# Products of two units at once and a new order of work in an adaLN block with a spectral filter and a SwiGLU FFN

## The chip, the cores and the metric

The kernel runs on one core of a Trainium2 chip. The core has five engines that run side by side, each in the order of its own instructions: TensorE (PE; its weight loads are listed as PEld), VectorE (DVE), ScalarE (ACT), GpSimd (POOL) and SyncE (SP), which here only issues transfers. They wait for one another on semaphores. The metric is the device time of one execution in microseconds (us); lower is better.

## The reference

One block of a transformer with adaptive layer norm. `x` is 2048 x 640, bf16.

```python
mod = (_silu(c) @ w_mod).reshape(c.shape[0], 6, 1, -1)
sa, ca, ga, sb, cb, gb = (mod[:, i] for i in range(6))
h = _layernorm(x) * (1 + ca) + sa
x = x + ga * irfft2(rfft2(h) * (w_r + 1j * w_i)).astype(bf16)     # over both axes
h = _layernorm(x) * (1 + cb) + sb
x = x + gb * ((_silu(h @ w_gate) * (h @ w_up)) @ w_down)          # 640 -> 1728 -> 640
```

## The kernel before

All work is matmuls with tables of cosines and sines. The 2048 rows lie as 16 tiles of 128, the 640 columns as 5 residues of 128. A stage is a set of small functions, one for each step of a tile or unit, and a string `plan` that lists their calls. The order of the plan is the order of the instructions on every engine: an engine never takes an instruction ahead of an earlier one in the plan. Which PSUM buffer a step gets is written out too, in `SLOTS1` and `SLOTS2` (three and four buffers of two banks), and `ON_DVE` names the evictions from PSUM that go to DVE; all others go to ACT. Below, a letter with a number is a call in the plan.

*Forward transform* (some 7 to 36 us). For each tile t: `T` turns x on PE (L301), `h` evicts it (L304), `G` forms a Gram matrix with two more columns of constants (L308), from which `d` takes variance and mean on DVE: a reduce along the diagonal (L313) and a small combination (L315). `p` and `r` make the reciprocal root for two tiles. `s` scales the table of the row transform by it, on POOL (L333, L334; tile 14 on DVE). `B` is the column transform (L340), `Z` evicts it with the mean taken out (DVE, L345), `S` is the row transform's first half (L353, L354) and `A` evicts it into `A_sb` (L367; tile 12 in three pieces, L362 to L364). At the end `J`, `Je` and `N` make turned and negated copies of the filter's weights W_r and W_i. Loads are calls in the plan too: `lx` (x, two tiles), `lg` (row table), `lW0` (W_i) and `lW1` (W_r, 1284 KB each), `lf` (rows of the weights' border), `lsa`, `lga`, `lK`, `lKI`, `lRi` (modulation weights and tables).

*Filter* (36 to 64 us). The 65 columns of the spectrum are 16 units of four and one single. `A_sb` is turned column by column into `B_all`: the first two units by PE (`T0`, `T1`, evicted by `t0`, `t1`, L506 and L507), the others by transposing transfers on SP's queue (`B2` to `B14`, `Bl`). `X` finishes the row transform of two units (L523, L531), `Xe` evicts one. `P` and `R` multiply a unit with W_r and W_i for 48 and 32 of its 80 rows (both L562; 768 and 512 elements). `a` adds the two planes of products on DVE for the units in `ADDED` (L570). `Y` turns the result on PE: 10 matmuls that add the planes (L586, L590), or 5 plain transposes where `a` has added them (L580, L581). `y` evicts (L599). `E` starts the inverse row transform (L611 to L624), `e` evicts into `Ep` (L634), `m` writes mirrored columns (`mirror`, L278). `ga` and `gt` make the gate `ga`, `gs` spreads it over the partitions, `Ri` scales the last table with it (L661).

*Inverse transform and first quarter of the FFN* (64 to 112 us). For each tile: `s` (L720), `V` (L727), `d` (L733), `x` adds the residual into `x1` (L736), `n` and `q` take mean and square sum (L740, L744). The first four tiles are normalized, turned (`T`, L772) and go through `g` (gate and up products, L812), `z` (silu, L817) and `m` (product into `AT`, L821). `sb`, `cb` and `mb` are modulation vectors of 25 small matmuls each (L241), `mt` turns the gate `gb` (L253) and has it spread over all partitions (L262), and `w` (`fold`, L848) multiplies a part of the down weights with it.

*The rest* (112 to 261 us). Down products of a quarter (L934, L921), then the next quarter's gate and up products, without a written plan. `x_out` adds x1 and stores. For the very last half tile the kernel uses two PSUM buffers of 160 columns, adds x1 there with two matmuls by the identity (L931), and evicts with ACT and DVE at once (L946).

Of the kernel before, what the change touches and what calls it, by code (L numbers as in the profile page):

```python
# [19 lines left out]
NI = 160  # L20
# [10 lines left out]
def _tables():  # L31
# [70 lines left out]
    "012021021021021020210210212012010210210210210"  # L102
)
SLOTS2 = (
    "0301321032103213012301230210321023102301230213201231032103210231023102310231320132012310321020130323"
    "013120132013201320132013201320132013201320132013201320132013201320132"
# [4 lines left out]
def adaln_block_kernel(  # L111
# [39 lines left out]
    one11 = const.tile([1, 1], BF16, name="one11")  # L151
    identb = const.tile([P, 128], BF16, name="identb")
# [29 lines left out]
    g_row = [dram.tile([1, D], BF16, name=n) for n in ("ga_row", "gb_row")]  # L182
    nc.vector.memset(one11[:], 1.0)
    nc.vector.memset(eps_t[:], EPS)
    nc.vector.memset(neg1[:], -1.0)
# [32 lines left out]
    def load_g(g):  # L218
# [5 lines left out]
             "lga": load(wm_g[:, :, 0:D], wm_v[:, :, 2 * D:3 * D]), "lRi": load(Rinv_sb[:], Rinv_dram), "lf": fix_rows}  # L224
# [58 lines left out]
    with tc.tile_pool(name="ph1", bufs=3) as ph1, \  # L283
# [33 lines left out]
        def root(t):  # L317
            n = GROUP[t]
            nc.scalar.activation(rstd1[:, t:t + n], vm[:, t:t + n, 0], ACT.Sqrt)
# [75 lines left out]

        cps = Tt[:, 330:330 + NC5]
        for k in range(NC5):
            nc.tensor.matmul(cps[:, k:k + 1], lhsT=c_row[0:1, k * 128:(k + 1) * 128], rhs=one11[:], start=True, stop=True)
        for _ in range(12):
            nc.tensor.matmul(Gt[:, 0:128], lhsT=identb[:], rhs=identb[:], start=True, stop=True)  # L400
# [44 lines left out]
        def negate(i):  # L445
# [5 lines left out]
        S_DVE, S_ACT, T_RING = (14,), (), (1, 2, 3, 4, 5, 6, 7)  # L451
        GROUP = {0: 2, 2: 2, 4: 2, 6: 2, 8: 2, 10: 2, 12: 2, 14: 2}
        plan = (
# [7 lines left out]
        )  # L461
        steps = {**LOADS, "ca": mod_ca, "cb": mod_cb, "rs": r_scaled, "rvp": rv_mm, "rv": rv_out, "T": turn, "h": turned, "G": sums,
# [13 lines left out]
    with tc.tile_pool(name="ph2", bufs=2, reuse_waits="tile") as ph2:  # L476
# [16 lines left out]

        def t2(u):
            ps = pss["t", u] = slot("t2ps")[:, 0, 0:320].bitcast(BF16)
# [97 lines left out]
        def copy_y(u):  # L593
            yf = pss.pop(("y", u))[:].rearrange("p b q -> p (b q)")
            if u in ADDED:
                yf = yf.bitcast(BF16)
# [425 lines left out]
```

## Time and profile before

| | us |
|---|---|
| median of 3 runs | 262.74 (262.62 to 265.64) |
| profiled execution | 262.81 |
| its span, first to last instruction | 261.0 |
| PE busy | 252.7 |
| DVE busy | 141.1 |
| ACT busy | 118.6 |
| POOL busy | 26.4 |

The granted TensorE clock was full throughout. In the timeline a row has start, duration, engine, line, operation, tiles and shapes, with the idle time before it in brackets; in a group (`x16 | 8.7, 550 | 0.0`) the busy time, the mean duration in ns and the idle time before follow the bars. A window's row has its length, then for each engine the busy time and the count of instructions, then clock, DMA share and GB/s. Busy time of PE holds the pipeline's tail of every matmul (a 128-column matmul is listed with 0.22 us), so distances from start to start say more.

### The profile page before, as it was taken

The page shows a single profiled execution, that of the slowest core. Times are in us where ns is not written, and L with a number is a line of the kernel's source. Part 1 is how long each engine was busy: PE and PEld are TensorE (multiplying, and loading weights), DVE is VectorE, ACT ScalarE, POOL GpSimd, SP SyncE. Part 2 cuts the span into 40 slices and gives each one's busy share as a digit, 9 for nine tenths or more (in the row PEclk, how much of TensorE's full clock was granted, in tenths as well). Part 3 has the DMA queues.
Part 4 walks back from the last instruction along what each step waited for, and adds up shares of the span by engine and source line. Part 5 has one row for each costly group of instructions (what it writes and reads, how often), then busy time and mean ns, then how long its engine had stood idle before and what let it go on. Part 6 is the DMA issues. An engine that isn't in the chain of part 4 may idle for free.

```text
span 261.0 us, 5283 instructions
## 1 busy us (share of the span) xinstructions
PE 252.7 (97%) x2168; PEld 159.9 (61%) x2172; DVE 141.1 (54%) x353; ACT 118.6 (45%) x212; POOL 26.4 (10%) x57
## 2 busy tenths in 40 slices
PE   6899999999999999999999999999999999999995
PEld 5788666888995444466544456744445664444664
DVE  5799989999887664933243343234344322433122
ACT  5689879996993669420222222032223103222000
POOL 4289700000010001300000000000000000000000
PEclk9999999999999999999999999999999999999999
DMA  7999499999599100141100040210005011000011
GB/s 243 381 356 298 112 175 160 176 330 379 153 370 303 38 14 1 23 77 57 58 10 3 0 92 11 75 35 10 3 0 100 30 48 35 10 3 0 0 53 50
DMA packets 36798, 27.88 MB, mean 107 GB/s; under 512 B 19493, under 2 KB 34214, under 8 KB 36646
## 3 DMA queue, kind: packets, MB, share of 16 engines
q1 hardware_dynamic: 36762, 27.54, 37.1%
q8 instruction: 17, 0.28, 0.5%
q14 instruction: 7, 0.06, 0.1%
q10 hardware_dynamic: 12, 0.00, 0.0%
HBM read 20.13 MB, written 2.62 MB: 87 GB/s over the span
## 4 chain that ended last, share of the span: by engine, by line
PE 79%; DVE 12%; ACT 3%; issue 2%; DMA 2%; SPq 1%; DVEq 0%; ACTq 0%
PE gu L812 37%; PE oa L934 21%; PE va L720 3%; DVE PP L562 3%; DMA x_sb<-in_A_x_dram 2%; PE oab L733 2%; PE gu L799 2%; ACT junk L744 2%; PE aps L353 1%; DVE AT L821 1%; PE aps L354 1%; PE z L340 1%; DVE Z L345 1%; PE gps L308 1%; DVE late L848 1%
## 5 line engine op out<-in xcount | busy, mean ns | idle before, releaser
L821 DVE TENSOR_TENSOR AT<-gu,sg 128x512 bf16<-128x512 f32 x52 | 35.7, 690 | 63.3 <-ACT sg L817 63.3
L812 PE MATMUL gu<-h2T_all,Wg 128*128 128x512 bf16 x260 | 64.6, 379 | 0.1
L812 PE MATMUL gu<-h2T_all,Wu 128*128 128x512 bf16 x256 | 63.7, 379 | 0.1
L817 ACT ACTIVATE sg<-gu 128x512 f32<-128x512 f32 x52 | 30.7, 596 | 67.9 <-PE gu L812 65.1
L934 PE MATMUL oa<-late,AT 128*128 128x320 bf16 x403 | 56.3, 299 | 0.5 <-DVE AT L821 0.5
L934 PEld LDWEIGHTS <-AT 128*128 128x128 bf16 x429 | 40.7, 98 | 17.6 <-issue 1.1
L812 PEld LDWEIGHTS <-Wu 128*128 128x128 bf16 x260 | 25.4, 98 | 30.7
L812 PEld LDWEIGHTS <-Wg 128*128 128x128 bf16 x260 | 25.3, 98 | 29.9
L948 DVE TENSOR_TENSOR xo<-oa,late 128x320 bf16<-128x320 f32 x31 | 13.4, 484 | 34.6 <-PE oa L934 18.2
L801 ACT ACTIVATE sg<-gu 64x512 f32<-64x512 f32 x4 | 2.4, 591 | 36.0 <-PE gu L799 36.0
L736 DVE SCALAR_TENSOR_TENSOR late<-oab,x_sb 128x640 bf16<-128x640 f32 x16 | 12.8, 822 | 6.4 <-PE oab L733 5.0
L333 POOL TENSOR_SCALAR Gs<-Gtab,rstd 128x256 bf16<-128x256 bf16 x15 | 13.9, 928 | 8.1 <-DVE rstd L323 7.1
L345 DVE SCALAR_TENSOR_TENSOR Z<-rtile,vm,z 128x640 bf16<-128x640 f32 x16 | 13.9, 871 | 0.1
L744 ACT ACTIVATE junk<-late,mean 128x640 bf16<-128x640 bf16 x16 | 13.3, 828 | 0.3
L367 ACT CAST A_sb<-aps 128x650 bf16<-128x650 f32 x15 | 10.6, 706 | 2.1 <-PE aps L354 2.0
L727 ACT CAST VT<-va 128x640 bf16<-128x640 f32 x16 | 10.2, 699 | 1.9 <-PE va L720 1.8
L720 PE MATMUL va<-Htab,Ep 128*128 128x128 bf16 x160 | 10.6, 219 | 0.1
L720 PEld LDWEIGHTS <-Ep 128*128 128x128 bf16 x160 | 9.5, 118 | 0.4 <-DVE Ep L278 0.3
L353 PE MATMUL aps<-Z,Gs 128*128 128x325 bf16 x32 | 9.2, 303 | 0.2 <-DVE Z L345 0.2
L354 PE MATMUL aps<-Z,Gs 128*128 128x315 bf16 x32 | 9.2, 298 | 0.0
L540 ACT CAST X<-xps 128x640 bf16<-128x640 f32 x13 | 8.5, 710 | 1.1 <-PE xps L531 0.8
L562 DVE TENSOR_TENSOR PP<-X,Wb 128x768 bf16<-128x768 bf16 x16 | 8.7, 550 | 0.0
(291 smaller groups left out, 307.0 us busy)
## 6 DMA issues: line engine op xcount, KB each, us to landing
x_sb<-in_A_x_dram SPq DMA_DIRECT2D x8, 320.0 KB
out_dram<-xo SPq DMA_DIRECT2D x15, 160.0 KB, 2.2
Wu<-in_B_w_up_dram SPq DMA_DIRECT2D x1, 2080.0 KB
late<-in_B_w_down_dram SPq DMA_DIRECT2D x1, 2080.0 KB
wm_g<-in_w_mod_dram SPq DMA_DIRECT2D x2, 800.0 KB
Wb<-in_A_w_r_dram SPq DMA_DIRECT2D x1, 1284.0 KB
Wb<-in_A_w_i_dram SPq DMA_DIRECT2D x1, 1284.0 KB, 13.0
Wg<-in_B_w_gate_dram SPq DMA_DIRECT2D x1, 1280.0 KB, 8.1
```

The lines of the kernel that those rows point to most:

```text
L333: e.tensor_scalar(Gss[t][:, 0:2], Gtab[:, t], rstd1[:, t:t + 1], None, ALU.mult)
L345: nc.vector.scalar_tensor_tensor(Zs[t][:].rearrange("p r q -> p (r q)"), rv, vm[:, t, 1:2], held.pop(("z", t))[:, 0:D], ALU.mult, ALU.add)
L353: nc.tensor.matmul(o, lhsT=Gs[:, a, :], rhs=Z[:, :, 0:NL], start=True, stop=False)
L562: nc.vector.tensor_tensor(bass.AP(o.tensor, o.offset, [o.ap[0], [4 * NI, 2], [2 * NI, 2], [4, n], [1, 4]]), bass.AP(xi.tensor, xi.offset, ...
L720: nc.tensor.matmul(vf[:, 128 * r:128 * r + 128], lhsT=Ep[:, t, 65 - 65 * g:193 - 65 * g, r], rhs=Htab[:, t, g, :], start=(f == 1 and r in ...
L736: nc.vector.scalar_tensor_tensor(x1[:, t, :].rearrange("p (a r) -> p a r", r=NR), VTs.pop(t).rearrange("p (r a) -> p a r", r=NR), 1.0, x_s ...
L744: nc.scalar.activation(junk[:], x1[:, t, :], ACT.Square, scale=-1.0 / D ** 0.5, bias=mean2[:, t, 1:2], accum_out=sq2[:, t:t + 1])
L812: nc.tensor.matmul(o, lhsT=w_[:, c5, fc * 128:(fc + 1) * 128], rhs=h2T(sc, c5), start=(c5 == 0), stop=(c5 == NC5 - 1))
L817: nc.scalar.activation(gus[fc][1][:], gus[fc][0][:, 0, :], ACT.Silu)
L821: nc.vector.tensor_tensor(AT[:, fc, :], gu[:, 1, :], sg[:], ALU.mult)
L934: nc.tensor.matmul(o, lhsT=AT[:, fc, tl * 128:(tl + 1) * 128], rhs=Wd_sb[:, fc, h * 320 + d0:h * 320 + d0 + n], start=(fc == 0 and not ear ...
L948: nc.vector.tensor_tensor(xos[tl][:, h * 320:(h + 1) * 320], ps[0][0], x_half(tl, h), ALU.add)
```

## The change

The products of the filter are made for a pair of units at once: X of two units lies in one tile with eight columns side by side, `P` and `R` take 1536 and 1024 elements, and `a` adds 1280. The unit that `Y`, `E` and `e` then work on is no longer four adjacent columns but the even or the odd ones of the pair's eight, so PE loads its weights from PP with a step of eight elements instead of four, and `e` writes every other column. `ADDED` is now the pairs 1 to 6 (12 units) instead of 8 units.

```diff
-            product_part(u, 48, 0, Wb[:, 1, NT - 1, 256 + 4 * u], 128)
+            product_part(u // 2, 48, 0, Wb[:, 1, NT - 1, 256 + 8 * (u // 2)], 128)
...
-                PPs[u] = ph2.tile([P, 2, NI, 4], BF16, name="PP", bufs=4)
+                PPs[p] = ph2.tile([P, 2, NI, 8], BF16, name="PP", bufs=2)
...
-                bass.AP(o.tensor, o.offset, [o.ap[0], [4 * NI, 2], [2 * NI, 2], [4, n], [1, 4]]),
+                bass.AP(o.tensor, o.offset, [o.ap[0], [8 * NI, 2], [4 * NI, 2], [8, n], [1, 8]]),
...
+            def planes(cp, b):
+                if b < 4:
+                    return PP[:, cp, 0:128, 2 * b + u % 2]
+                return PP[:, cp, 128:NI].rearrange("p q j -> p (q j)")[:, u % 2:256:2]
...
-                copy(bass.AP(o.tensor, o.offset, [o.ap[0], [65 * NR, 2], [193 * NR, NT], [NR, n], [1, NR]]),
+                copy(bass.AP(o.tensor, o.offset, [o.ap[0], [65 * NR, 2], [193 * NR, NT], [2 * NR, n], [1, NR]]),
...
-        ADDED = (0, 2, 4, 6, 8, 10, 12, 14)
-        MCOLS = ((0, 15), (15, 31), (31, 47), (47, 59), (59, 63))
+        ADDED = (1, 2, 3, 4, 5, 6)
+        MCOLS = ((0, 15, 1), (15, 31, 1), (31, 55, 1), (55, 62, 2), (56, 63, 2))
```

The two border transposes are split by tile of origin: `T0` takes the eight blocks of `A_main`, `T1` the two of `A_rest`, each with one eviction (1024 and 256 elements) instead of two.

In the forward transform the square sums of four tiles move from PE and DVE to ACT (a new call `k`); their Gram matmuls keep only the two constant columns.

```diff
+        def squares(t):
+            nc.scalar.activation(wm_sb[:, 0], x_sb[:, t, :], ACT.Square, scale=5.0 / D ** 0.5, accum_out=ssq[:, t, 0:1])
...
         def sums(t):
+            c0 = 128 if t in SQ else 0
             for r in range(NR):
-                nc.tensor.matmul(Gt[:, 0:130], lhsT=hT_all[:, t, r, 0:128], rhs=hT_all[:, t, r, 0:130],
+                nc.tensor.matmul(Gt[:, c0:130], lhsT=hT_all[:, t, r, 0:128], rhs=hT_all[:, t, r, c0:130],
...
         def stats(t):
+            if t in SQ:
+                nc.vector.scalar_tensor_tensor(vm[:, t, :], Gt[:, 129:131], Gt[:, 128:129], ssq[:, t, :], ALU.mult, ALU.add)
+                return
...
+        SQ = (8, 9, 12, 13)
...
+        keep_busy(Tt, 9)
```

`keep_busy` are matmuls of zeros ahead of the first real ones. All three plans and both slot strings are new, and so is `ON_DVE`:

```diff
-        "A12 Xe0 Xe9 Xe10 Xe16 e1 e14 e15 f0 f1 f2 f3 f4 f6 f7 f8 f9 g15 h0 t0 t1 y0 y2 y4 y8 y12 y14 y16 "
+        "A13 Xe0 Xe10 Xe16 f0 f1 f2 f3 f4 f6 f7 f8 f9 g15 h0 h1 h7 h14 t0 t1 t16 y2 y4 y8 y9 y11 y12 y13 y15 y16 "
```

In the new plans W_i is loaded ahead of x tiles 12 to 15 and the W_r load (`lx10 lg8 ... lW0 ... lx12 lg10 ... lx14 lg12 lg14 ... lW1 ... lsa`); `lga`, `lKI` and `lRi` come in the forward transform, the weights of cb and sb as `lcb` and `lsb` among the transposing transfers (`B10 ... lcb B12 ... B14 ... lsb`). The filter starts with `T0 T1 t0 t1 X0 B2 Xe1 B4 Xe0 Bl2 R1 B6 P1 X2 ...` and ends with `... Ri e15 E14 E16 e13 m0 m1 e16 e14 m2 m4 sb m3 L4 cb`: sb and cb, with their copies to SBUF, stand there instead of in the next stage, and `Ri` stands ahead of the mirrors. The inverse stage reads

```diff
-        "sb s0 V0 s1 s2 sx d0 x0 V1 s3 s4 V2 d1 d2 n0 V3 s8 V4 x1 s5 q0 x2 d3 cb n1 x3 n2 V8 V5 d4 q1 cx n3 q2 d5 x4 q3 x5 s7 "
+        "s0 s1 V0 V1 s11 s3 s2 d0 lb x0 V11 s7 V3 n0 d1 V2 s4 x1 d2 V7 x2 s5 q0 d3 n1 V4 n2 x3 V5 q2 d11 x11 mb d5 d7 n3 q1 s6 "
...
+        "f6 f7 f8 f9 n6 s8 n5 d13 V10 q6 x13 V8 g4 d9 d10 x9 n9 g6 z4 mt m4 n4 q9 x10 gA z6 n11 n7 m6 d12 g5 q7 q11 d15 g3 x12 "
+        "w2 d8 x15 z5 g0 z0 m5 z3 n13 n10 g2 n12 m0 d14 m3 g1 z2 q5 x14 g7 n14 n15 x8 z1 m2 w3 q12 mA n8 q10 z7 w0 q14 q13 q4 "
```

where `lb` and `lw` stand for the loads of wm_gb and of Wg and Wd. The later folds are spread, and the last one follows the last product:

```diff
-    folds = {8: (4, 5, 6), 9: (7,), 10: (8,), 11: (9, 10, 11), 12: (12, 13)}
+    folds = {8: (4, 5), 9: (6, 7), 10: (8, 9), 11: (10, 11), 12: (12,), 13: (13,)}
...
             ffn_mul(AT, fc)
+            if sc == 0 and fc == NFC - 2:
+                for f in folds[13]:
+                    fold(f)
```

At the very end the last half tile is computed as two parts one after the other, without the identity matmuls; DVE adds x1 to each, and each part is stored by itself.

```diff
-                for o, d0, n in ps:
-                    nc.tensor.matmul(o, lhsT=identb[:], rhs=x_half(tl, h)[:, d0:d0 + n], start=True, stop=False)
...
+            nc.vector.tensor_tensor(xos[tl][:, d0:d0 + n], o, x1[:, t, d0:d0 + n], ALU.add)
...
+        if sc == 3:
+            part = parts(3, 1)[1]
+            down(3, 1, part)
+            down13(3, 1, part)
+            x_out(3, 1, part)
```

More of the change, by code (lines that the diff above doesn't have):

```diff
@@ L394, in rv_out, with keep_busy @@
             nc.scalar.activation(rv, held["rv"][:, 0:D], ACT.Copy, scale=0.2)
+        def keep_busy(ps, n):
+            for _ in range(n):
+                nc.tensor.matmul(ps[:, 0:128], lhsT=hot[:], rhs=hot[:], start=True, stop=True)
         cps = Tt[:, 330:330 + NC5]
+        keep_busy(Tt, 9)
         for k in range(NC5):
             nc.tensor.matmul(cps[:, k:k + 1], lhsT=c_row[0:1, k * 128:(k + 1) * 128], rhs=one11[:], start=True, stop=True)
-        for _ in range(12):
-            nc.tensor.matmul(Gt[:, 0:128], lhsT=identb[:], rhs=identb[:], start=True, stop=True)
+        keep_busy(Gt, 12)
         nc.scalar.activation(sc_f[:], cps, ACT.Silu)
@@ L955, in adaln_block_kernel @@
             for h in range(2):
-                down(tl, h)
+                down(tl, h, parts(tl, h)[0])
         for tl in range(4):
             for h in range(2):
-                if tl < 2 or early(tl, h):
-                    down13(tl, h)
+                down13(tl, h, parts(tl, h)[0])
         for tl in range(2):
             for h in range(2):
-                x_out(tl, h)
+                x_out(tl, h, parts(tl, h)[0])
         for tl in range(2, 4):
             for h in range(2):
-                down(tl, h)
-                if not early(tl, h):
-                    down13(tl, h)
-                if sc == 3 and tl == 3:
-                    x_out(tl, h)
-            if sc < 3 or tl == 2:
-                for h in range(2):
-                    x_out(tl, h)
+                down(tl, h, parts(tl, h)[0])
+            for h in range(2):
+                x_out(tl, h, parts(tl, h)[0])
+        if sc == 3:
[3 more added lines that the diff above has]
+            x_out(3, 1, part)
 @with_exitstack
```

164 lines of the change are left out of this document (76 added, 88 removed), and 30 rows, old and new, of the table plan.

## The prediction

> **What bounds the kernel now.** I read the page first, then the stages, then the chain that ended last, then each engine's own timeline inside a stage.
>
> ```profile
> GB/s 243 381 356 298 112 175 160 176 330 379 153 370 303 38 14 1 23 77 57 58 10 3 0 92 11 75 35 10 3 0 100 30 48 35 10 3 0 0 53 50
> ```
> ```profile
> core 0 of [0], span 261.0 us
> core 0: us, PE busy (x) PEld busy (x) DVE busy (x) ACT busy (x) POOL busy (x), PEclk, DMA share, GB/s
> 7.50:36.63 29.13, 27.76 (x369) 22.61 (x370) 27.22 (x92) 25.30 (x44) 18.86 (x30) 1.00 0.87 269
> 36.63:64.20 27.57, 26.80 (x437) 22.19 (x436) 26.41 (x64) 23.91 (x42) 0.00 (x0) 1.00 1.03 252
> 64.20:112.20 48.00, 47.31 (x449) 30.30 (x453) 35.37 (x94) 33.96 (x69) 4.49 (x6) 1.00 0.44 135
> ```
> ```profile
> 2.66 4.79 DMA x_sb<-in_A_x_dram
> ...
> 90.67 4.33 PE gu L812 x20
> ```
>
> Four stretches. Up to 7.5 us the kernel waits for the second pair of x tiles (the DMA on the chain); the change leaves the loads ahead of that pair as they are, so this stretch stays. From 7.5 to 36.63 (forward transform) and from 36.63 to 64.2 (filter) DVE is the fullest engine: 27.22 of 29.13 us and 26.41 of 27.57. ACT has 49.21 us of work in these 56.70, DVE 53.63, or 94.6%. PE looks as full, but its busy time counts the tail of every matmul, so it is an upper bound. From 64.2 to 112.2 (inverse transform and the first quarter of the FFN) DVE and ACT have room and PE is back to back: there only PE's instructions count. After 112.2 the three other quarters run on PE alone, which the change does not touch, except for the last tile.
>
> The profiled execution took 262.81 us, 1.81 more than its span, and 0.07 more than the median of the runs shown (262.74). The sum below is made against 262.81.
>
> **Forward transform.** Durations overlap a little on one engine, so I price by spacing from start to start.
>
> ```profile
> 13.80 0.29 DVE L313 CUSTOM_DVE_ANT_0 junk<-gps,identb 128x128 bf16<-128x128 f32 x1
> 14.02 0.08 DVE L313 DVE_READ_ACCUMULATOR2_ANT ssq<- 128x1 f32 x1
> 14.14 0.22 DVE L315 SCALAR_TENSOR_TENSOR vm<-gps,ssq 128x2 f32<-128x2 f32 x1
> ```
> ```profile
> 17.42 0.71 ACT L367 CAST A_sb<-aps 128x650 bf16<-128x650 f32 x1
> 18.14 0.69 ACT L304 COPY early<-t1ps 128x640 bf16<-128x640 bf16 x1
> 18.73 0.71 ACT L367 CAST A_sb<-aps 128x650 bf16<-128x650 f32 x1
> ```
> ```profile
> 97.82 0.83 ACT L744 ACTIVATE junk<-late,mean 128x640 bf16<-128x640 bf16 x1
> ...
> 98.78 0.83 ACT L744 ACTIVATE junk<-late,mean 128x640 bf16<-128x640 bf16 x1
> ```
>
> For tiles 8, 9, 12 and 13 DVE loses the diagonal reduce: 14.14 - 13.80 = 0.34 us, four times, -1.36. ACT gains four squares with an accumulator; none runs in this stage, but L744 is the same operation on the same shape: 98.78 - 97.82 = 0.96, four times, +3.84. Two transposed tiles (h7, h14) go from ACT (0.59) to DVE (0.40, as its 640 bf16 elements below): ACT -1.18, DVE +0.80. Tile 12's eviction in three pieces goes to ACT and tile 13's in one piece to DVE; ACT pays some 0.2 more (three starts instead of one), DVE saves about as much. The border transposes come out in two copies instead of four; three starts at about 0.1 against one more, -0.2 on DVE. Sum: DVE -1.0, ACT +2.9. The narrowed Gram matmuls (2 columns for 130, 20 of them, at most 0.03 each) free PE by 0.5, hidden while ACT and DVE set the pace. The nine zero matmuls and two memsets stand ahead of 7.5 us, behind the wait for x: nothing, and at most their own microsecond if x came earlier.
>
> W_i (1.31 MB) now stands ahead of x tiles 12 to 15. Summing the GB/s slices (6.5 us each), the 3.9 MB up to and with tile 12 arrive at about 12.7 us, with W_i ahead 5.2 MB at about 16.4. Tile 12's turn is the thirteenth group of five on L301:
>
> ```profile
> 19.06 0.44 PE L301 MATMUL t1ps<-identb,x_sb 128*128 128x128 bf16 x5
> ```
>
> So the delay is hidden by 2.7 us; every microsecond beyond would stop PE at T12 with all later transposes and products behind it. The tables that move from the filter stage into this one follow W_r, in slices that fall to 112 GB/s, so there is room. In the filter stage the load lcb (0.82 MB, 2.5 us at 330 GB/s) now stands on SP's queue between the transposing transfers B10 and B12. X12 comes two pairs of units after X8 (27.57 / 8, or 3.4 us, a pair): hidden; without that cover X12 would wait the 2.5 us, and PE with it.
>
> **Filter.**
>
> ```profile
> 38.09 0.56 DVE L562 TENSOR_TENSOR PP<-X,Wb 128x768 bf16<-128x768 bf16 x1
> 38.56 0.42 DVE L562 TENSOR_TENSOR PP<-X,Wq 128x512 bf16<-128x512 bf16 x1
> 38.90 0.55 DVE L562 TENSOR_TENSOR PP<-X,Wb 128x768 bf16<-128x768 bf16 x1
> ...
> 39.70 0.48 DVE L570 TENSOR_TENSOR PP<-PP 128x640 bf16<-128x640 bf16 x1
> 40.10 0.42 DVE L562 TENSOR_TENSOR PP<-X,Wq 128x512 bf16<-128x512 bf16 x1
> ```
> ```profile
> 61.85 0.81 DVE L634 CAST Ep<-eps__1464 128x640 bf16<-128x640 f32 x1
> 62.65 0.50 DVE L634 CAST Ep<-eps__1490 128x320 bf16<-128x320 f32 x1
> 63.06 0.48 DVE L634 CAST Ep<-eps__1491 128x320 bf16<-128x320 f32 x1
> ```
>
> The headline edit is worth little. A 768-element product costs 0.47, a 512-element one 0.34: 0.51 ns an element and only 0.08 fixed. Sixteen pairs cost 16 x 0.81 = 12.96; eight at double length cost 8 x (0.86 + 0.60) = 11.68: -1.28. The listed duration (0.55 against 0.42) would have promised twice that. The sum of planes costs 0.40 for 640 and, by the same slope, 0.73 for 1280; six of these instead of eight small ones: 6 x 0.73 - 8 x 0.40 = +1.18. So products and sums together are even on DVE, and what they buy is on PE: four more units use 5 transposes instead of 10 matmuls.
>
> The evictions change hands. DVE gives up Xe9 (0.80, as the f32 tile above), e1 and e14 (0.80 each), half of e15 (0.41): -2.81. It takes y9, y11, y13 (0.40 each, bf16) and y15 (0.80, f32) for y0 and y14 (0.40 each), and t16 (0.2): +1.40. The scaling of Rinv, which ran behind the last mirror, now stands ahead of it: +0.75. DVE in all: -1.28 + 1.18 - 2.81 + 1.40 + 0.75 = -0.8. ACT, at 0.65 for such a tile (between its 0.59 and 0.72): Xe9 +0.65, two y less -1.30, e1, e14 and the half of e15 +1.65, t16 -0.3, two small modulation copies +0.3: +1.0.
>
> Unknown here: evictions that write runs of 5 or 4 elements with gaps (E, X). The nearest rows are e14 (runs of 20, 0.81 long) and the A eviction of 650 (0.71); if all of that 0.10 were the gaps' and came once more, on some 30 tiles, it would be 3 us, mostly ACT's. I take 0.2 for ACT, near the other end, since two engines and not the runs explain most of the 0.10; shorter runs are no reason for a gain. The mirror's pieces with a step: 0 to 0.3, and I take 0.
>
> Both stages together: DVE 53.63 - 1.8 = 51.8, ACT 49.21 + 3.9 + 0.2 = 53.3. **The bound changes hands**, from DVE at 53.63 to ACT at 53.3. At the same 94.6% filling, 53.3 needs 56.3 us: -0.4. Two engines within 1.5 us of each other stall one another more than one did, so I take **-0.2**, with -1.8 (the larger engine at 97%) and +1.6 (at 91.4%) as ends.
>
> **The weights' step.** For Y the loads of PP step over 8 elements instead of 4.
>
> ```profile
> L720 PEld LDWEIGHTS <-Ep 128*128 128x128 bf16 x160 | 9.5, 118 | 0.4 <-DVE Ep L278 0.3
> L586 PEld LDWEIGHTS <-PP 128*128 128x128 bf16 x66 | 4.3, 114 | 0.3
> L590 PEld LDWEIGHTS <-PP 128*128 128x128 bf16 x16 | 1.2, 98 | 0.0
> ```
>
> Side by side 98 ns, step 4 114, step 5 118: about 0.02 ns per byte spanned, so step 8 (2048 bytes) about 135 ns. The loads overlap each other and the matmuls, so this stays hidden, as the 118 does now: 160 loads of Ep are 9.5 us of busy time, 59 ns apiece. I take nothing; the upper end is a rival below. [...]
>
> **Inverse transform and first quarter.**
>
> ```profile
> 69.14 0.93 PE L241 MATMUL mg_ps<-sc_col,wm_g 128*128 128x64 bf16 x25
> ...
> 112.22 0.99 PE L934 MATMUL oa<-late,AT 128*128 128x320 bf16 x6 [0.49 <-DVE AT L821]
> ```
>
> The 25 matmuls of the cb modulation leave this PE-bound stretch: 0.93 less the tail of the last, 0.78. They go to the end of the filter, behind those of sb, where PE waits for e13, e16, e14 and the mirror (ACT: two of 0.65 and a short one). sb and cb are 1.6 there, so they fit about, with 0.25 sticking out: **-0.5**. If ACT were earlier, all 0.78 would stick out. In the closing gap PE waits 0.49 for AT(12), behind which fold 13 now stands, and fewer folds stand ahead: **-0.45**. The new order must not stop PE elsewhere. The places are mb, which needs wm_gb (loaded once sb is done), and the folds, which need the gate's broadcast:
>
> ```profile
> 81.12 0.22 PE L253 MATMUL gT_ps<-identb,gb_col 128*5 128x128 bf16 x1
> ...
> 84.85 0.35 SPq L262 DMA_DIRECT2D gb_bc<-gb_row  x1
> ```
>
> From turning the gate to issuing its broadcast took 3.7 us; first in line is now w2, called after g4, g6, mt, gA, d12, earlier behind mt than before. DVE may stand there 2 us with x15, m5, m0 behind it; PE's g0 waits for x15's PSUM slot. I put +0.1 on the stage. Wg's load is free to go once cb is done, so earlier than now; I count no gain, since PE stands back to back where it is first used.
>
> **Tail.**
>
> ```profile
> 255.78 0.30 PE L931 MATMUL ob<-late,identb 128*128 128x160 bf16 x2
> 255.91 1.96 PE L934 MATMUL ob<-late,AT 128*128 128x160 bf16 x26
> ```
>
> The two matmuls that added x go: -0.13, from the one start to the next. The last half is added by one DVE instruction instead of copied by two engines, at the same 160 columns: 0. The last store carries half the bytes: 0 to -0.2. **-0.15**.
>
> **Sum:** 262.81 - 0.2 - 0.5 - 0.45 + 0.1 - 0.15 = 261.6; against the median, 0.07 lower: **261.5 us**. (A measurement of this kernel tells about 2%, 5.3 us, from no change.)
>
> **Rivals.** (1) *ACT's load eats the front's gain*: 53.3 us of ACT at 91.4% filling, front +1.6, the rest -1.0: 263.4. For it: squares at 0.96 replace reduces at 0.34. Against: ACT's waits now are for PE and DVE, which get lighter. Chance 0.20. (2) *The new order packs well*: front -1.8, an inverse stage without stalls -1.4, tail -0.2: 259.4. For it: POOL and PE gain room. Against: 97% on an engine with many producers. 0.18. (3) *Slower: strided weights are not hidden.* If the 80 loads with step 8 run one after the other at 135 ns instead of the 56 ns of a 128-column matmul, PE gains 6.3 us in the filter, less 1.1 for 20 matmuls gone. With PE's 26.80 as an upper bound it would hold 32.0 of a stage of 27.57: +4.4, and 262.81 + 4.4 - 1.0 = 266.2. It decides once the loads cost PE 1.9 us more, 24 ns each. Against it: Ep's loads. 0.06. (4) *The broadcast or W_i comes late*: DVE stands at w2, or PE at T12, for 2 us more than I gave: 263.5. 0.08. (5) *The merge does nothing*: if a double instruction costs two single ones (0.94, 0.68, 0.80), DVE has 53.5 and ACT 53.3; two full engines stall each other more, front +0.4: 262.2. Against it: the same 0.51 ns an element holds between two lengths. It lies inside the forecast's range.
>
> The forecast, with (5), has 0.48: 260.4 to 262.6. With (1), (2) and (4) the range is 259.0 to 264.2; (3) lies outside. Faster by over 2% (under 257.5) needs all stages at their best ends: 0.03. Slower by over 2% (over 268.0) needs (3) with more: 0.03. Else 0.94.
>
> **What would show it.** Products at 0.86 and 0.60 from start to start; L586-like loads at about 135 ns and matmuls still 56 ns apart; ACT busier than DVE in the first two stages; no gap ahead of AT(12) at the end of the first quarter; 25 fewer matmuls after the filter; the span from the end of the filter to the first oa about 47.1 us. Wrong would be: Y's matmuls over 70 ns apart, DVE still the fuller engine, idle PE time behind w2, mb or T12.

## The result, and the profile after

The changed kernel takes **263.97 us** (median, 263.44 to 266.04) where the kernel before, run beside it, takes 262.81: a ratio of **1.004**, with a 95% interval of 1.0022 to 1.0058. It is slower, by about 1.2 us; I had forecast 1.2 us less. The difference is small, 0.4%, but the interval lies clear of 1. The profiled execution took 264.6, with a span of 262.7. Device times of other runs below come with the median of the kernel before from the same session, which lay between 262.88 and 263.31.

The stretches after, cut at the second pair's turn, at X0 and at PE's last wait for E's mirror (columns as in the prediction, whose first cut, 36.63, lies 0.40 behind X0; ahead of them the first two before, cut at X0):

```profile
7.50:36.23 28.73, 27.36 (x365) 22.29 (x365) 26.82 (x91) 24.90 (x44) 18.86 (x30) 1.00 0.87 271
36.23:64.20 27.97, 27.20 (x440) 22.51 (x440) 26.81 (x65) 24.31 (x43) 0.00 (x0) 1.00 1.02 251
```
```profile
8.59:36.98 28.39, 27.01 (x364) 21.92 (x365) 26.27 (x79) 26.22 (x52) 19.46 (x30) 1.00 0.92 285
36.98:65.82 28.84, 27.78 (x446) 23.03 (x446) 26.50 (x45) 26.50 (x45) 0.00 (x0) 1.00 0.96 237
65.82:114.15 48.33, 47.24 (x428) 29.62 (x429) 34.20 (x93) 33.66 (x67) 4.44 (x6) 1.00 0.37 120
```

ACT's work has grown to equal DVE's in both first stretches, and the third is not shorter though 25 matmuls have left it. The difference of the two profiled executions, stretch by stretch, up to DVE's last instruction (the last store behind it takes 2.5 us in both):

| stretch | before | after | difference | my sum |
|---|---|---|---|---|
| start to the turn of the second pair of x tiles | 7.50 | 8.59 | +1.09 | 0 |
| forward transform, to the border's first turn (T0) | 27.58 | 26.94 | -0.64 | -0.2 with the filter |
| T0 to X0 | 1.15 | 1.45 | +0.30 | in that -0.2 |
| filter, X0 to PE's last wait for E's mirror | 27.97 | 28.84 | +0.87 | +0.28 (sb, cb) |
| inverse transform and first quarter, to the down product that needs AT(12) | 48.02 | 48.33 | +0.31 | -1.13 |
| the rest, to DVE's last instruction | 146.26 | 146.05 | -0.21 | -0.15 |

The first row is the DMA piece at the head of the chain that ended last, 4.79 us before:

```profile
2.75 5.79 DMA x_sb<-in_A_x_dram
```

It moves from run to run. In four profiles with the old warm-up the second pair was turned at 7.50, 7.81, 7.91 and 7.92; in 16 with the new one at 7.50 to 9.35, 8.08 in the mean. Most of the 1.09 is therefore one execution's luck; whether 0.3 of it belongs to the change, these runs don't settle. The sum of the other rows is +0.63.

At the filter's end the chain that ended last now runs over ACT's evictions of E, and from them over DVE's mirror to PE:

```profile
61.65 1.88 ACT Ep L655 x3
...
63.76 0.70 ACT Ep L655
```

ACT's timeline a little earlier, where several of them stand in a row, and ahead of it two from the kernel before (L634); then, at the filter's end, DVE's and PE's rows:

```profile
57.30 0.75 ACT L634 CAST Ep<-eps__1362 128x640 bf16<-128x640 f32 x1
57.91 0.76 ACT L634 CAST Ep<-eps__1378 128x640 bf16<-128x640 f32 x1
```
```profile
56.66 1.04 ACT L655 CAST Ep<-eps__1318 128x640 bf16<-128x640 f32 x1
57.37 1.05 ACT L655 CAST Ep<-eps__1331 128x640 bf16<-128x640 f32 x1
58.07 1.06 ACT L655 CAST Ep<-eps__1340 128x640 bf16<-128x640 f32 x1
58.79 1.08 ACT L655 CAST Ep<-eps__1347 128x640 bf16<-128x640 f32 x1
```
```profile
64.50 1.27 DVE L283 TENSOR_SCALAR Ep<-Ep,neg 128x1920 bf16<-128x1920 bf16 x3 [0.97 <-ACT modcols L679]
```
```profile
65.82 1.37 PE L743 MATMUL va<-Htab,Ep 128*128 128x128 bf16 x21 [0.73 <-DVE Ep L283]
```

From start to start an eviction takes 0.70 to 0.72 us, where the kernel before took 0.61. DVE waits 0.97 us for ACT before the last three mirror pieces (the releaser named is a small copy next to e14), and PE 0.73 for them.

### The profile page after: what moved, and what is told of

It reads as the page before. It is cut to its first block, busy times and chain, and to the rows that moved or that the text cites. A ratio compares the mean times of both kernels' runs of the same rounds, so it can differ in the third digit from the quotient of the medians.

```text
span 262.7 us, 5238 instructions
## 1 busy us (share of the span) xinstructions
PE 254.1 (97%) x2159; PEld 160.4 (61%) x2159; DVE 140.5 (53%) x328; ACT 120.8 (46%) x219; POOL 27.0 (10%) x57
## 4 chain that ended last, share of the span: by engine, by line
PE 81%; ACT 8%; DVE 4%; DMA 2%; issue 2%; SPq 1%; ACTq 0%; DVEq 0%
PE gu L835 38%; PE oa L945 21%; PE va L743 3%; ACT junk L767 3%; DMA x_sb<-in_A_x_dram 2%; ACT Ep L655 2%; PE z L352 2%; PE aps L365 2%; ACT X L558 2%; PE gu L822 2%; PE aps L366 2%; PE oab L756 1%; PE gps L317 1%; DVE AT L844 1%; PE yps L609 1%
## 5 line engine op out<-in xcount | busy, mean ns | idle before, releaser
L835 PE MATMUL gu<-h2T_all,Wu 128*128 128x512 bf16 x260 | 64.6, 379 | 0.0
L945 PE MATMUL oa<-late,AT 128*128 128x320 bf16 (+1 forms) x416 | 57.3, 297 | 0.7 <-DVE AT L844 0.7
L956 DVE TENSOR_TENSOR xo<-oa,late 128x320 bf16<-128x320 f32 (+1 forms) x32 | 13.7, 479 | 34.6 <-PE oa L945 19.1
L345 POOL TENSOR_SCALAR Gs<-Gtab,rstd 128x256 bf16<-128x256 bf16 x15 | 14.5, 964 | 8.4 <-DVE rstd L335 8.2
L767 ACT ACTIVATE junk<-late,mean 128x640 bf16<-128x640 bf16 x16 | 13.2, 827 | 1.2 <-DVE mean L763 0.9
L379 ACT CAST A_sb<-aps 128x650 bf16<-128x650 f32 x14 | 9.9, 714 | 1.1 <-PE aps L366 0.9
L558 ACT CAST X<-xps 128x640 bf16<-128x640 f32 x14 | 9.5, 742 | 0.5 <-PE xps L549 0.5
L799 ACT ACTIVATE h2T_all<-h2T_all,modcols,one_p_cb 128x512 bf16<-128x512 bf16 x6 | 4.6, 805 | 8.4 <-DMA h2T_all<-xn2c 8.4
```

Source lines behind the costliest of these rows:

```text
L345: e.tensor_scalar(Gss[t][:, 0:2], Gtab[:, t], rstd1[:, t:t + 1], None, ALU.mult)
L558: evict("Xe%d" % u)(Xs[u // 2][:, :, 4 * (u % 2):4 * (u % 2) + 4].rearrange("p q (b j) -> p q b j", b=2), xps[:, :, 0:2 * NI].rearrange("p ...
L767: nc.scalar.activation(junk[:], x1[:, t, :], ACT.Square, scale=-1.0 / D ** 0.5, bias=mean2[:, t, 1:2], accum_out=sq2[:, t:t + 1])
L835: nc.tensor.matmul(o, lhsT=w_[:, c5, fc * 128:(fc + 1) * 128], rhs=h2T(sc, c5), start=(c5 == 0), stop=(c5 == NC5 - 1))
L945: nc.tensor.matmul(o, lhsT=AT[:, fc, tl * 128:(tl + 1) * 128], rhs=Wd_sb[:, fc, h * 320 + d0:h * 320 + d0 + n], start=(fc == 0 and not ear ...
L956: nc.vector.tensor_tensor(xos[tl][:, d0:d0 + n], o, x1[:, t, d0:d0 + n], ALU.add)
```

## The experiments

**The gaps in E.** First the changed kernel once more:

> The changed kernel once more, to see which of its differences repeat. Its trace showed the second pair of x tiles landing 1.09 us later than before (8.54 against 7.45), with the same loads ahead of it. If that belongs to the change (the nine zero matmuls or the memsets ahead of it), it shows again: first T of that pair at 8.5, ratio 1.004. If it is the luck of one execution, the pair lands near 7.5 here, and the rest of the kernel adds up to what the other stages show: forward 0.8 shorter, border copy 0.4 longer, filter 0.9 longer, inverse 0.3 longer, tail 0.2 shorter, so +0.6 us and a ratio near 1.002.

263.79 us (beside 262.98), ratio 1.003, 1.0013 to 1.0048. T0 to X0 is 1.45 again, the filter 28.88, the third stretch 48.34, and x is late again (8.76). Then E's columns side by side. The table of the last transform stays as it is, so the result has its columns in another order:

```diff
-  [193 * NR, NT], [2 * NR, n], [1, NR]]
+  [193 * NR, NT], [NR, n], [1, NR]]
...
-  put(8 * (u // 2) + u % 2 - 1, 0, 4)
+  put(4 * u - 1, 0, 4)
```

> The changed kernel, with E's columns written side by side again instead of every second one (the columns of the filtered spectrum then stand in another order, so the output is another one). Theory: ACT's evictions of E became slower by the gaps, from 0.61 to 0.72 us from start to start, and 14 of them in an ACT-bound filter are the filter's loss: evictions back at 0.61, filter 28.84 down to about 27.9, time 263.0 (0.9 less than the changed kernel). Rival: the new order alone (ACT full with what moved to it) holds the filter: evictions get shorter, but PE or DVE then ends last and the time stays at 263.8 to 264.1. Second rival: the evictions are longer for another reason (all three engines on the memory at once): they stay at 0.72.

262.57 us in the same session: **1.22 less** than the changed kernel (ratio to the kernel before 0.9983, 0.9965 to 1.0002). ACT's timeline:

```profile
55.56 0.75 ACT L655 CAST Ep<-eps__1318 128x640 bf16<-128x640 f32 x1
56.16 0.76 ACT L655 CAST Ep<-eps__1331 128x640 bf16<-128x640 f32 x1
56.76 0.77 ACT L655 CAST Ep<-eps__1340 128x640 bf16<-128x640 f32 x1
```

The spacing is 0.60, and PE's wait for the mirror is gone. With E's columns the last two mirror pieces lose their step too and fall from 0.63 us together to 0.53; that is a small part of the 1.22, and `e_backwards` below has these pieces dense as well. The same edit the other way round, in the kernel before:

> The kernel before, with E's columns written every second one, as in the changed kernel, and nothing else (the columns of the filtered spectrum then stand in another order, so the output is another one). Theory of the gaps: E's evictions on ACT go from 0.61 to 0.72 us, those on DVE (e1, e14, e15) may too; ACT has 3.7 us of room in this filter, DVE 1.2, so the time grows by 0.2 to 0.9: 263.0 to 263.7. Rival (the gaps cost nothing by themselves): evictions at 0.61, time 262.8.

263.76 us (beside 262.98), 0.78 more: a ratio of 1.0031, 1.001 to 1.0053. Its ACT shows the same lengthening, 1.05 where the kernel before had 0.75:

```profile
57.64 1.05 ACT L634 CAST Ep<-eps__1362 128x640 bf16<-128x640 f32 x1
58.35 1.07 ACT L634 CAST Ep<-eps__1378 128x640 bf16<-128x640 f32 x1
```

So the writing of E by itself makes either kernel slower, and more so where ACT is fuller. Gap or short run? With no gap left, but each group of columns written from its last to its first (against the changed kernel, cut):

```diff
-  o, i = Ev[:, 0, 0, s0, 0], ps[...]
+  o, i = Ev[:, 0, 0, s0 + n - 1, 0], ps[...]
...
-  [193 * NR, NT], [2 * NR, n], [1, NR]]
+  [193 * NR, NT], [-NR, n], [1, NR]]
```

> As after_e_close (columns side by side, no gaps), but each group of columns written from its last to its first: runs of 10 bytes, each behind the run written after it, with no gap left (the columns of the filtered spectrum stand in another order, so the output is another one). If the short runs by themselves cost ACT the time, E's evictions are as with the gaps (0.72 us apart, 850 to 1110 ns) and the time is 263.8. If it is the gaps (each piece of memory only half written), they are at 0.61 and the time at 262.6.

263.78 us (beside 263.11), ratio 1.0018, 0.9987 to 1.0048. The rows show more than the time:

```profile
57.76 1.16 ACT L655 CAST Ep<-eps__1318 128x640 bf16<-128x640 f32 x1
58.54 1.18 ACT L655 CAST Ep<-eps__1331 128x640 bf16<-128x640 f32 x1
```

All of them stand 0.76 to 0.80 from the next, without a gap. So it doesn't take holes to make the evictions longer; what both forms share are the runs of five elements (10 bytes). That the runs are the cause is argued, not shown: a backward step in longer runs was not tried, and it may cost by itself.

**The front.** The new forward transform ahead of the old filter, inverse transform and tail:

> The forward transform of the changed kernel (its order, squares on ACT, its warm-up, W_i early), with the filter, the inverse transform and the tail of the kernel before; the three tables that the new order loads early are loaded there and no more in the filter. If the 0.78 us that the forward stage gained are real and the late pair of x was luck: 262.0 (ratio 0.997). If the late pair belongs to the change: 263.1 (1.001). If the forward gain is only bought by work left for the filter: 262.8, with the filter longer by what the forward stage is shorter.

262.70 us (beside 262.98), ratio 0.9985, 0.9968 to 1.0001: nearest the third case. The forward stretch is 26.95 as in the changed kernel, but X0 starts at 36.15, 28.65 after the second pair's turn, where it was 28.73 before: from T0 to X0 it takes 1.70, so 0.55 of the 0.63 gained is gone at the seam. With the old filter's order the second turn stands behind the first copy, and PE waits for ACT, which copies Wq later than before:

```profile
35.87 0.44 PE L514 MATMUL t2ps<-identb,A_sb 128*128 128x128 bf16 x5 [0.98 <-ACT Wq L458]
```

The squares taken off ACT again (`SQ = ()`, and no `k` in the plan):

> The changed kernel with the squares of all tiles taken from the Gram matrix on DVE, as before (no squares on ACT). DVE gets 4 times 0.34 us more, ACT 4 times 0.96 us less, PE's narrow Gram matmuls are wide again. If the squares on ACT are what made the forward stage 0.6 us shorter, the stretch from the second pair's first turn to the border's first grows from 26.95 to 27.3 to 27.6, and the time by 0.4 to 0.6. If ACT was the fuller engine there, it shrinks by up to 0.5.

265.39 us (beside 263.31), ratio 1.0069, 1.0045 to 1.0092. The forward stretch was 28.85 us, but PE had turned the second pair at about half its pace in that execution (ten turns in 1.05 us instead of 0.59), so the same kernel ran once more:

> no_squares once more: its profiled execution had PE at half its pace from 8.4 to about 11 us (ten turns in 1.05 us, 0.59 in the changed kernel), so the 28.85 us of its forward stretch holds some 0.6 that is not the squares'. If the squares carry the gain of the forward stage, an execution without that slow start shows 28.0 to 28.4 (26.95 with them) and the median stays 1.0 to 1.6 above the changed kernel's 263.8 to 264.0. If most of the 1.9 was the slow start, it shows 27.0 to 27.6 and a median of 264.0 to 264.6.

265.25 us (beside 263.11), ratio 1.0079, 1.0052 to 1.0105. The forward stretch, with the changed kernel's below it:

```profile
7.76:36.02 28.26, 27.26 (x353) 21.99 (x355) 26.30 (x86) 22.71 (x41) 19.59 (x30) 1.00 0.90 285
```
```profile
8.59:35.53 26.94, 26.29 (x354) 21.37 (x355) 24.91 (x77) 24.78 (x49) 19.46 (x30) 1.00 0.91 290
```

1.32 us more in the stretch (28.26, the first case), and 1.3 to 1.5 in the time, beside 263.97 and 263.79 of the changed kernel in other sessions. DVE has 1.39 more work, PE with its wide Gram matmuls 0.97 more, ACT 2.07 less: ACT does not set this stage. DVE and PE weren't separated. In this order the squares carry more than the whole gain.

**The border.** With two copies for each tile, as before (the plan left as it is):

> The changed kernel with the border turned as before: each of the two tiles has its own five transposes and two copies (512 and 128 columns), the plan as it is. Theory: X0 needs only the first tile's copies and could start ahead of the second's; the one copy of 1024 columns took 0.70 us on DVE and made X0 wait for all of it. T0 to X0 goes from 1.45 back to about 1.15, the time from 263.8 to 263.5. Rival: X0 waits for something that runs beside it (DVE's negation of Wq, ACT's copies of Wq), then T0 to X0 stays at 1.4 and the time too; or DVE, which gets three more instructions of some 0.1, gives the 0.3 back in the filter.

263.78 us (beside 263.31); T0 to X0 1.42. The one piece alone is not what made the seam longer. Nor is it the order of calls:

```diff
-  "T0 T1 t0 t1 X0 B2 ...
+  "T0 t0 T1 t1 X0 B2 ...
```

> As border_two (the border in two tiles with copies of 512 and 128 columns), and the first copies called right behind the first tile's transposes (T0 t0 T1 t1 X0 instead of T0 T1 t0 t1 X0), as in the kernel before. Theory: the order made the seam longer, since X0 stands behind all copies; T0 to X0 goes from 1.42 to 1.15, the time from 263.78 to 263.5. Rival: DVE's earlier work (the evictions of the last transform tiles, dsa, the negation of Wq) sets it, then it stays at 1.4 and the time at 263.8.

264.04 us (beside 262.88), T0 to X0 still 1.42. Moving the negation of Wq behind the copies (`close_folds_v_n`, below) left it at 1.45.

The traces show why each of these edits had to fail: X0 waits for two things that end together. Rows of the changed kernel, and X0 in `border_two`:

```profile
35.91 1.91 ACT L459 CAST Wq<-wps 128x1024 bf16<-128x1024 f32 x2
36.98 0.73 PE L541 MATMUL xps<-Ktab,B_all 128*128 128x160 bf16 x8 [0.73 <-DVE B_all L525]
```
```profile
35.92 0.71 PE L540 MATMUL xps<-Ktab,B_all 128*128 128x160 bf16 x8 [0.70 <-DVE B_all L523]
```

In the changed kernel DVE's copy of 1024 columns ends at 36.92 and the first of these two copies of Wq on ACT at 36.90. In `border_two` the first tile's two copies on DVE (35.03, 0.42 us, and 35.37, 0.21 us) end by 35.58, but X0's first matmul starts at 35.92. The DVE copy that the row names ends only with the start, at 35.92; ACT's copy ends at some 35.86 there, an estimate: 36.90 less the 1.04 us by which the second pair was turned earlier (7.55 against 8.59). The new slot string gives X0 the buffer 3 that this copy empties; in the old one X0 has the buffer of T0, and T1 has buffer 3, which is the wait for ACT in `front_only`. By that estimate the one piece and the slot string each hold the seam at 1.42 to 1.45. A run with both taken back was not made.

**The inverse transform.** Its order, slots and folds as before, with sb and cb still in the filter:

> The changed kernel with the order of the inverse transform, its slots and its folds as before (the modulations of sb and cb stay in the filter; the loads of wm_gb and Wg stand behind s0 and d3). Theory: the new order cost the stage what the 25 matmuls that left it had saved: five tiles of s ahead of the first d leave DVE idle for 3.3 us, then its sums x1 stand back to back and PE waits for their slots (0.7 to 0.8 us in five gaps near 69 to 73 us). With the old order the stretch from the end of the filter to the first down product that needs AT(12) goes from 48.3 to about 47.3 (48.02 less 0.78), the time to 262.9. Rival: the waits come from moving sb and cb (other slots, loads that collide), then it stays at 48.0 to 48.4 and the time at 263.5 to 263.9.

263.75 us (beside 263.31). From PE's wait for the mirror to its wait for AT(12)

```profile
65.05 1.15 PE L743 MATMUL va<-Htab,Ep 128*128 128x128 bf16 x17 [0.72 <-DVE Ep L283]
...
113.05 5.20 PE L942 MATMUL oa<-late,AT 128*128 128x320 bf16 x37 [0.49 <-DVE AT L844]
```

is 48.00 us: to 0.02 the time of the kernel before, which had 25 matmuls more. The old order shortens the stage by 0.33 and the time by nothing (263.78 in border_two, same session), so it is not what took the 0.78, and PE's work alone does not set this stage's end. The chain that ended last shows what does, in the changed kernel and in the kernel before, where it ends with the PE row at 112.22 (L767 and L744 are square sums, `sg` is the SiLU):

```profile
98.80 0.60 ACT sg L840
...
106.26 0.49 ACT sg L840
106.77 0.69 DVE AT L844
...
114.15 5.61 PE oa L945 x40
```
```profile
95.03 0.61 ACT sg L817
...
104.33 0.49 ACT sg L817
104.85 0.69 DVE AT L821
```

In both the chain leaves PE some 15 to 17 us before the end of the stage. It runs mostly over ACT, where seven square sums of some 0.95 us each stand among the SiLUs, then over DVE. The prediction shows the row just ahead of it (90.67, PE) and stops there. DVE's part, in the changed kernel and then in the kernel before (AT(8) first, AT(12) last; L865 and L848 are folds):

```profile
106.77 0.69 DVE L844 TENSOR_TENSOR AT<-gu,sg 128x512 bf16<-128x512 f32 x1 [3.61 <-ACT sg L840]
107.38 0.88 DVE L865 TENSOR_TENSOR late<-late,gb_bc 128x640 bf16<-128x640 bf16 x2
...
109.50 0.88 DVE L865 TENSOR_TENSOR late<-late,gb_bc 128x640 bf16<-128x640 bf16 x2
...
111.61 0.89 DVE L865 TENSOR_TENSOR late<-late,gb_bc 128x640 bf16<-128x640 bf16 x2
...
113.02 0.48 DVE L865 TENSOR_TENSOR late<-late,gb_bc 128x640 bf16<-128x640 bf16 x1
113.42 0.68 DVE L844 TENSOR_TENSOR AT<-gu,sg 128x512 bf16<-128x512 f32 x1
```
```profile
104.85 0.69 DVE L821 TENSOR_TENSOR AT<-gu,sg 128x512 bf16<-128x512 f32 x1 [0.24 <-ACT sg L817]
105.46 0.48 DVE L848 TENSOR_TENSOR late<-late,gb_bc 128x640 bf16<-128x640 bf16 x1
...
107.17 0.48 DVE L848 TENSOR_TENSOR late<-late,gb_bc 128x640 bf16<-128x640 bf16 x1
...
108.88 1.28 DVE L848 TENSOR_TENSOR late<-late,gb_bc 128x640 bf16<-128x640 bf16 x3
...
110.69 0.88 DVE L848 TENSOR_TENSOR late<-late,gb_bc 128x640 bf16<-128x640 bf16 x2
111.49 0.68 DVE L821 TENSOR_TENSOR AT<-gu,sg 128x512 bf16<-128x512 f32 x1
```

Both have **seven folds** between AT(8) and AT(12): 2, 2, 2, 1 and 1, 1, 3, 2. From AT(8) to AT(12) it is 6.65 and 6.64 us. This part starts when ACT's SiLU releases AT(8), and ahead of that DVE of the changed kernel stands idle for 3.61 us. So the folds should stand there (moving ACT's square sums was not tried):

```diff
-  folds = {8: (4, 5), 9: (6, 7), 10: (8, 9), 11: (10, 11), 12: (12,), 13: (13,)}
+  folds = {8: (4, 5, 6, 7, 8, 9), 9: (10,), 10: (11,), 12: (12,), 13: (13,)}
```

> The changed kernel with folds 4 to 9 all ahead of AT(8), one fold each behind AT(8) and AT(9) as (10) and (11), then 12 and 13 as they are. Theory: DVE's chain that makes the last AT late begins at AT(8), which waits for ACT; between AT(8) and AT(12) stood seven folds before and stand seven folds now, so the chain could not get shorter; ahead of AT(8) DVE idles. With three folds in between the 0.69 us gap ahead of the first down product that needs AT(12) goes, the time falls by 0.7 to 263.1. Rival: the gap hangs on ACT's last SiLU or on the normalised tiles, then it stays at 0.5 to 0.7 and the time at 263.8.

262.97 us (beside 263.31), 0.8 less than border_two and inverse_order in the same session. PE no longer waits for AT(12). The same in the kernel before:

> The kernel before with folds 4 to 9 ahead of AT(8), then one fold behind AT(8) and one behind AT(9), then 12 and 13 ahead of AT(12). Theory: its gap of 0.49 us ahead of the first down product that needs AT(12) has the same cause as the 0.69 of the changed kernel (seven folds between AT(8) and AT(12)); with four there it goes and the time falls by 0.5 to 262.5. Rival: the gap is ACT's, then the time stays at 262.9 to 263.1.

262.88 us (beside 263.13), ratio 0.9962, 0.9936 to 0.9989. By the medians that is 0.25 less, half of what I expected and at the edge of the rival; the ratio says more. PE's wait falls from 0.49 to 0.18, not to nothing: there AT(8) waited for ACT by only 0.24, so the folds put ahead of it delay it.

Do the 25 matmuls of cb in the kernel before stand in a stretch where PE waits anyway?

```diff
+  if name == "cb":
+      for q in range(NC5):      # 5 matmuls instead of 25
+          nc.tensor.matmul(..., start=True, stop=True)
+      return
```

> The kernel before with 5 of the 25 matmuls of the cb modulation in the inverse transform (one of its five terms; 20 matmuls of 31 ns less, 0.62 us of PE). Theory: they stand in a stretch in which PE waits for slots that ACT and DVE free, so holes take their place: time within 0.2 of 262.9, holes between 69 and 75 us longer by 0.4 to 0.6. Rival (my prediction): the stretch is PE's, the time falls by 0.6 to 262.3.

263.52 us (beside 263.11), ratio 0.9997, 0.9964 to 1.0031: nothing gained. But the reason is partly another than either theory's. PE ran into the load of the next modulation's weights:

```profile
72.22 0.95 PE L241 MATMUL mg_ps<-sc_col,wm_gb 128*128 128x64 bf16 x25 [0.80 <-DMA wm_gb<-in_w_mod_dram]
```

Those matmuls covered that load, besides the slots.

**Together.** E's columns side by side, with the rows of the inverse table in that order, and the folds early:

```diff
+  at = np.arange(1, 64)
+  row = row[np.concatenate([[0], at // 8 * 8 + at // 4 % 2 + 2 * (at % 4)])]
```

> The changed kernel with two of its losses taken back together: E's columns side by side, with the rows of the inverse table put in the same order (so that the output is what the reference asks for), and folds 4 to 9 ahead of AT(8). If the two are independent, the time is 262.57 (columns side by side alone) less 0.8 (folds alone): 261.75, under the kernel before by 1.2. If the earlier filter only makes the rest wait for the same loads or engines, it stays above 262.3.

**261.54 us** (beside 263.13), ratio **0.9937**, 0.9909 to 0.9966: faster than both. PE goes into the down products without a wait:

```profile
109.68 7.23 PE L947 MATMUL oa<-late,AT 128*128 128x320 bf16 x52
```

Two attempts to close the remaining holes of PE near 70 us, by giving DVE evictions of V:

> As close_folds, with the evictions of V of tiles 1 and 11 (the second and third of the inverse transform) on DVE instead of ACT. Theory: the 25 matmuls that left the inverse transform stood in a stretch where PE waits for ACT's evictions and DVE's sums to free its slots, so the holes between 69 and 74 us (0.8 us more of them than before) took their place; two evictions less on ACT (1.3 us), put where DVE idles, close 0.3 to 0.7 of them: 261.1 to 261.4. Rival: DVE's sums alone set that pace, then the holes stay and the time is that of close_folds or 0.2 more.

263.45 us (beside 263.13), a miss: V of tile 11 stands behind x0 on DVE's queue, and PE waited 1.67 us for it. With the negation of Wq moved as well:

> As close_folds_v, with the negation of Wq (0.74 us on DVE, just ahead of the border's copies) put behind these copies. Theory: X0 waits 0.7 us for the border's copies because DVE does this negation first, so T0 to X0 falls from 1.45 to about 0.8 and the time by 0.4 to 0.6. Rival: the first products on DVE need Wq and the next X needs slots from ACT, so the filter takes back what X0 gains: no change within 0.2.

263.60 us (beside 263.13), the same miss. With tiles 0 and 1, ahead of x0:

> As close_folds, with the evictions of V of tiles 0 and 1 on DVE, where they stand ahead of the first sum x0 (in close_folds_v, V of tile 11 stood behind x0 and PE waited 1.67 us for it). Theory: ACT, two evictions (1.3 us) ahead, closes 0.3 to 0.7 of the holes between 69 and 74 us: 260.8 to 261.2. Rival: DVE's sums, back to back from 66.7 to 72.6 us, set the pace there, then the holes stay and the time is 261.4 to 261.7.

261.39 us (beside 263.11), ratio 0.9922, 0.9894 to 0.995. By PE's starts, less its instructions at their usual spacing, the holes between 63 and 80 us are about 1.25 in all, as in close_folds. The holes stayed, as the rival had it. With the old border on top:

> close_folds_v01 with the same border. If the seam's 0.3 us carry through the filter: 261.1; if the filter takes them back (ACT's copies of Wq and the first X of the slots): 261.3 to 261.5.

261.65 us (beside 262.88), ratio 0.9949, 0.9925 to 0.9972: no further gain. T0 to X0 is 1.42 there too, so this run doesn't test what a shorter seam brings.

## Why the prediction was wrong, step by step

**The step that failed first: "I take 0.2 for ACT, near the other end, since two engines and not the runs explain most of the 0.10."** The term was mis-sized: 0.2 us, where the spacing went from 0.60 to 0.72 on 14 whole tiles of ACT and parts of two, 1.7 us of ACT's time, of which 1.22 us reached the time (0.78 in the kernel before, whose ACT had room). The argument about the 0.10 was right in itself: it lay between the engines, since ACT takes 0.60 for a tile in runs of 20 and 0.59 for the A eviction. But it says nothing of runs of five, which no row had, and I took its smallness for theirs. X, by contrast, costs the same with its new writes. Its group in after_e_close (new X), then in front_only (old X):

```profile
L558 ACT CAST X<-xps 128x640 bf16<-128x640 f32 x14 | 9.3, 708 | 0.5 <-PE xps L549 0.5
```
```profile
L556 ACT CAST X<-xps 128x640 bf16<-128x640 f32 x13 | 8.5, 711 | 1.7 <-PE xps L547 1.7
```

**The second: "fewer folds stand ahead", -0.45.** The count was taken over the stage, not over the chain. Fold 13 went behind AT(12), but another moved from ahead of AT(8) to behind it, so seven stayed; the gap grew from 0.49 to 0.69. Moving them for real brought 0.8.

**The third: "there only PE's instructions count", -0.5 for cb.** The stage kept its length with 25 matmuls less, whichever order stood (48.00 and 48.33 against 48.02): the chain to its end ran over ACT's square sums and DVE, and near its start PE waited for others. I had read the room of DVE and ACT from their sums over the whole stage. With the folds early some of the gain appeared: from the first s to the down product that needs AT(12), 48.60 with E side by side alone fell to 47.62 in close_folds (the row of 52, whose first twelve, 0.136 apart, don't need it). The kernel before took 48.57, and 48.27 with its folds early, so with early folds in both the change is worth 0.65 here. It needed an edit that the change does not contain.

These steps cover most of the miss of 2.4 us: taking back the writes of E (1.22) and the folds (0.8) gives 261.54. That this meets the 261.5 is in part luck, since the other terms were off both ways.

**Right in kind.** Products and sums on DVE: 0.61, 0.87 and 0.73 from start to start, as worked out (0.60, 0.86, 0.73). The long rows, by group:

```profile
L578 DVE TENSOR_TENSOR PP<-X,Wb 128x1536 bf16<-128x1536 bf16 x8 | 7.6, 948 | 0.0
L578 DVE TENSOR_TENSOR PP<-X,Wq 128x1024 bf16<-128x1024 bf16 x8 | 5.5, 683 | 0.1
L586 DVE TENSOR_TENSOR PP<-PP 128x1280 bf16<-128x1280 bf16 x6 | 4.9, 813 | 0.0
```

The strided weights:

```profile
L609 PEld LDWEIGHTS <-PP 128*128 128x128 bf16 x60 | 4.2, 140 | 0.9 <-issue 0.2
L612 PEld LDWEIGHTS <-PP 128*128 128x128 bf16 x40 | 2.6, 138 | 0.0
```

138 to 140 ns against 135 forecast, and Y's matmuls 61 to 63 ns apart (medians) instead of 56, some 0.6 us of PE in all: rival (3), which needed 24 ns each, did not come. In these rows a step of eight is a little dearer than four: a load takes 24 to 26 ns more (114 ns before), and the matmuls stand 5 to 7 ns further apart. W_i early stopped nothing, DVE waited 0.2 us for the broadcast of the gate, and the last row of the table gave 0.21 for 0.15.

**The forward stage** went my way (-0.64), though not by my account: "the bound changes hands" failed there. The squares are worth 1.3 us, about DVE's four reduces at full price, and ACT's 2.07 us more took none of it back that could be seen; the rest of the new order gave some of it back, and the seam to the filter 0.30 more, where I had counted a gain. The square's price of 0.96 was too high: three of the four stood 0.72 to 0.74 us from the next instruction (L744 has `mean` as a further input). **Rival (1)**, ACT's load eats the gain, lies near with 263.4, but named the front: it was the filter, and the writes rather than the number of instructions. Rival (4) lies as near with 263.5, but nothing of it came. "ACT busier than DVE" did not come: they are level, 26.22 against 26.27 and 26.50 against 26.50.

## What to carry to other kernels

Price an eviction by the shape of what it writes, not by its element count alone: here 128x640 on ACT cost 0.60 us in runs of 20 elements and 0.72 in runs of five with gaps. Where a new layout cuts the runs short, take the long end, or reorder a table at the far side instead. Follow the chain to a stage's end before counting on its engines' room, and count the work that hides a stall from the event that starts that chain, not over the stage. Here matmuls taken out of a stretch brought nothing until the engine that ended it was relieved too.

## What the runs showed of the hardware

ACT's evictions of E, 128x640 from f32 to bf16, stand 0.60 us apart in runs of 20 elements (`after_e_close`), 0.70 to 0.73 in runs of five with gaps (the changed kernel), 0.76 to 0.80 in runs of five written backwards into dense columns (`e_backwards`). Runs of four elements at a step of eight cost nothing in X (708 ns in `after_e_close` against 711 in `front_only`). Why five differ from four was not tried. DVE hardly minds: its half eviction of E (128x320) takes 526 ns and 0.42 us to the next start with gaps (the changed kernel), 485 and 496 ns and 0.40 to 0.41 us without (the kernel before). The first loads of x vary between executions: the second pair was turned at 7.50 to 9.35 us, a spread of 1.9. And in some executions PE turned them at about half its pace: in e_backwards ten turns took 1.05 us from start to start instead of 0.59, and the granted clock (the number ahead of the last two) was 0.57:

```profile
8.00:12.00 4.00, 3.52 (x31) 3.34 (x33) 1.73 (x11) 2.20 (x5) 0.84 (x1) 0.57 1.05 379
```

Its forward stretch took 28.06 us for the same instructions that took 26.95 elsewhere. A turn took 0.105 us there against 0.059, and PE's two waits just ahead were 0.67 and 0.44 us. In `no_squares` ten turns took 1.05 us too, and the granted clock reads 1.00 there (8 to 12 us). What slows these turns was not shown. So a stretch of one profile is compared only after a look at the spacing of PE's rows at its start.
